# A chunked state-space scan and a gated feed-forward network on one core: the first loads in another order, GpSimd's scaling moved ahead of the second weights, a scan split in two

## The chip, the cores and the metric

The kernel runs on one core of a Trainium2 chip. A core has five engines with instruction queues of their own: TensorE (PE in the profile; its weight loads are listed as PEld), VectorE (DVE), ScalarE (ACT), GpSimd (POOL) and SyncE (SP, which here only starts transfers). Sixteen DMA engines move the data. The metric is the device time of one execution in microseconds; a lower time is better.

## The reference

There are two stages. The first is a recurrence over 768 tokens for each of 4 batches and 8 heads, with head dimension 32 and state dimension 16, written in chunks. The second is a feed-forward network with a ReLU gate over all 3072 tokens, of width 256 and inner width 1536.

```python
for c in range(nc):
    cum = np.cumsum(la, axis=-1)                               # la = log a in the chunk
    L = np.exp(cum[:, :, :, None] - cum[:, :, None, :]) * causal
    M = np.einsum('bhin,bhjn->bhij', Cc, Bc) * L
    y_intra = np.einsum('bhij,bhjd->bhid', M, xc)
    y_inter = np.einsum('bhin,bhnd->bhid', Cc, state) * np.exp(cum)[:, :, :, None]
    y[:, :, sl] = y_intra + y_inter
    Bx = np.einsum('bhjn,bhjd->bhjnd', Bc, xc) * decay_from_j[...]
    state = decay_full[:, :, None, None] * state + np.sum(Bx, axis=2)
...
gate = np.maximum(x @ w_gate, 0.0)      # x: y as 3072 tokens x 256
val = x @ w_val
return gate * val @ w_out
```

Inputs and output are float32 in HBM; the matmuls run on bfloat16 copies.

## The kernel before, in words

The kernel is free to choose its own chunk length and takes 128 tokens. Two chunks, 256 tokens of one batch with all 8 heads, are a *pair*; there are 12 pairs, three to a batch. Two pairs are a *block* of 512 tokens for the feed-forward network; there are 6 blocks. The feed-forward network of a block needs the recurrence of its two pairs, and the recurrence of the next pairs is woven between its matmuls, so that TensorE always has work.

The order of the work on each engine is the order of the program: `in_order` at the end ties each instruction to the one before it on its engine. Between engines only semaphores count. So the text of the kernel from line 620 on is a schedule, written by hand. Transfers are issued by SP (nearly all loads and stores), by ScalarE (four loads at the start) and by GpSimd (the weights, which are turned from float32 to bfloat16 on their way). An instruction that waits holds up all that stands behind it on its engine, a transfer's issue too.

The steps of a pair, with their lines in the kernel before:

- **Loads.** `load_bc` (L86) and `load_x` (L96) load B, C and x of the pairs 0 to 2, which are laid out in a special way ("wide"); `load` (L114, L115) loads the other pairs. `a_sb` (L134) is the decays of all batches, `a0` (L121) those of batch 0.
- **Scaling.** `scale_wide(p, j, engine)` (L276) multiplies C (j = 1) or B (j = 0) by decay factors `wfac` and writes the bfloat16 tile bs, in two instructions. Pair 0 is scaled on VectorE, pairs 1 and 2 on GpSimd. The factors are copied from PSUM for C, and made by a reciprocal for B. `cast_x` (L303) turns x to bfloat16 (xb).
- **Transposes.** `turn` and `transp` (L320) on TensorE, then `tevac` copies the result to BT (L335, L345) and, with a mask, to CT (L338 on ScalarE, L341 on VectorE).
- **Scores.** `G_wide` (L357) makes four PSUM banks of C times B. Two of them VectorE multiplies by the causal mask straight from PSUM (`gmask` with `True`, L370); the other two ScalarE copies to SBUF first (`gcopy`, L374), and `gmask` then masks them there.
- **State.** `adds` (L391) sums B times x of each chunk, `carry` (L410) and `pass_on` (L419) carry the state on with `dec`; `inter_wide` (L431) adds the state's part to y and `D_wide` (L445) the part within the chunk. `yevac_wide` (L455) copies y to yT, the input of the feed-forward network.
- **Feed-forward.** `gv` (L563, L566, 512 tokens) and `gvh` (L581, 256 tokens) do the gate and value products of 128 inner columns, ScalarE makes r by ReLU (L569, L584), VectorE makes h from r and the value product (L570, L587), and `fout` (L599) multiplies h by `wo`. PSUM has five shared banks, handed out in turn; a half-step `gvh` takes one, `gv` two, `G_wide` four.
- **Weights.** `weights(f0, f1)` (L192) issues wg and wv for the inner columns f0 to f1 of 12, `weights_out` (L196) all of wo. A one-element copy (`gate`, L634) that reads a factor holds the first of them back.
- **Decays of batches 1 to 3.** Two scans over `a_sb` (L232), a reciprocal and a multiply (`middle`, L238, L239), the matmuls of `decay` (L247).
- `keep_warm` (L183) runs matmuls on a tile of zeros whose result nobody reads.

Of the kernel before, what the change touches and what calls it, by code (L numbers as in the profile page):

```python
# [29 lines left out]
def kernel(  # L30
# [48 lines left out]
    def load_bc(p, j, *qs):  # L79
        s = st.setdefault(p, {})  # L80
        if "bcr" not in s:
            s["bcr"] = raw.tile([128, NH, 2, 2, N], FP32, tag="bcr", name="bcr")
        n = NH // len(qs)
        for i, q in enumerate(qs):
            hs = slice(i * n, (i + 1) * n)
            q.dma_start(  # L86
                out=s["bcr"][:, hs, j].rearrange("p h r n -> p h (r n)"),
                in_=(B, C)[j][0, hs, p * 256:(p + 1) * 256, :].rearrange(
                    "h (p r) n -> p h (r n)", r=2))

    def load_x(p, *qs):
        xr = raw.tile([128, NH, 2, D], FP32, tag="xr", name="xr")
        n = NH // len(qs)
        for i, q in enumerate(qs):
            hs = slice(i * n, (i + 1) * n)
            q.dma_start(out=xr[:, hs].rearrange("p h r d -> p h (r d)"),  # L96
                        in_=x[0, hs, p * 256:(p + 1) * 256, :].rearrange(
                            "h (p r) d -> p h (r d)", r=2))
        st.setdefault(p, {})["xr"] = xr

    def load(p):
        q = nc.sync
        if p < NWIDE:
            load_bc(p, 1, q)
            load_bc(p, 0, q)
            load_x(p, q)
            return
        b, c0 = p // PPB, 2 * (p % PPB)
        xr = raw.tile([128, 2, NH, D], FP32, tag="xr", name="xr")
        bcr = raw.tile([128, 2, 2, NH, N], FP32, tag="bcr", name="bcr")  # L110
        for i in range(2):
            sl = slice((c0 + i) * 128, (c0 + i + 1) * 128)
            for src, j in ((B, 0), (C, 1)):
                q.dma_start(out=bcr[:, i, j], in_=src[b, :, sl, :].rearrange("h s n -> s h n"))  # L114
            q.dma_start(out=xr[:, i], in_=x[b, :, sl, :].rearrange("h s d -> s h d"))  # L115
        st[p] = {"xr": xr, "bcr": bcr}
# [8 lines left out]
    nc.vector.memset(first, 0.0)  # L125
    load_bc(0, 1, nc.sync, nc.scalar)
    load_bc(0, 0, nc.sync, nc.scalar)
    load_bc(1, 1, nc.sync)
    load_bc(1, 0, nc.scalar)
    load_x(0, nc.sync, nc.scalar)  # L130
    nc.scalar.activation(first[:, 1:2], first[:, 0:1], AF.Relu)
    load_x(1, nc.sync)
    a_sb = glob.tile([2 * BH, H], FP32)
    nc.sync.dma_start(out=a_sb, in_=a.rearrange("b h (w s) -> (b h w) s", w=2))  # L134
    load(2)
    load(3)

    identf = const.tile([2 * BH, 2 * BH], FP32)
    make_identity(nc, identf)
# [37 lines left out]
    def keep_warm(n, tag="shared"):  # L177
        if tag == "tp":
            w = mm.tile([128, 128], FP32, tag="tp", name="w")
        else:  # L180
            w = bank("w", (128, 128))
        for _ in range(n):
            nc.tensor.matmul(out=w, lhsT=warm, rhs=warm, start=True, stop=True)  # L183
# [5 lines left out]
    def weights(f0, f1):  # L189
        fs = slice(f0 * 128, f1 * 128)  # L190
        for w, src in ((wg, moe_w_gate), (wv, moe_w_val)):
            nc.gpsimd.dma_start(  # L192
                out=w[:, :, fs], in_=src[:, fs].rearrange("(k p) f -> p k f", k=2))
# [74 lines left out]
    def scale_wide(p, j, eng):  # L268
        s = st[p]
        if "bs" not in s:  # L270
            s["bs"] = bs = att.tile([128, 4, 128], BF16, tag="bs", name="bs")
            s["tin"] = [[bs[:, 2 * j + r] for r in range(2)] for j in range(2)]
        src = s["bcr"].rearrange("s (t q) j r n -> s j r t q n", t=2)[:, j]
        f = wfac[:, j, :, :, p]
        for t in range(2):
            eng.tensor_tensor(  # L276
                out=s["bs"][:, 2 * j:2 * j + 2].rearrange(
                    "s k (q t n) -> s k t q n", q=4, t=2)[:, :, t],
                in0=src[:, :, t],
                in1=f[:, :, 4 * t:4 * t + 4].to_broadcast([128, 2, 4, N]),  # L280
                op=ALU.mult)
# [16 lines left out]
    def cast_x(p, ceng):  # L298
        s = st[p]
        cast = ceng.copy if ceng is nc.scalar else ceng.tensor_copy  # L300
        xb = att.tile([128, 2 * NH * D], BF16, tag="xb", name="xb")
        if p < NWIDE:
            cast(xb, s["xr"].rearrange("s h r d -> s (h r d)"))  # L303
            s["xb"] = xb.rearrange("s (h r d) -> s h r d", h=NH, r=2)
        else:
            cast(xb, s["xr"].rearrange("s i h d -> s (i h d)"))
            s["x"] = [xb[:, i * NH * D:(i + 1) * NH * D] for i in range(2)]

    def transp(p, k, apart=False):

        s = st[p]
        if "tp" not in s:
            s["tp"] = {}
        if apart and k == 0:
            s["tp"][k] = bank("tpb", (128, 2, 128), BF16)
        elif not s["tp"]:
            tp = mm.tile([128, 2, 2, 128], BF16, tag="tp", name="tp")
            s["tp"] = {0: tp[:, 0], 1: tp[:, 1]}
        for i in range(2):
            nc.tensor.transpose(out=s["tp"][k][:, i], in_=s["tin"][k][i], identity=ident)  # L320
# [61 lines left out]
    def adds(p):  # L382
        y_wide(p)
        s = st[p]
        s["A"] = [s["yw"][i][:, 256:320] for i in range(2)]
        halves = [i for i in range(2) if 2 * p + i < NC - 1]
        for r in range(2):
            for i in halves:
                half = slice(64 * i, 64 * i + 64)
                for q in range(4):  # L390
                    nc.tensor.matmul(  # L391
                        out=s["A"][i][32 * q:32 * q + 32],
                        lhsT=s["bs"][half, r, 32 * q:32 * q + 32],
                        rhs=s["xb"].rearrange("s (t q) r d -> s q r t d", t=2)[half, q, r],
                        start=r == 0, stop=True,
                        tile_position=(64 * i, 32 * q), skip_group_check=True)
        for i in halves:
            s["begun"][i] = True
# [4 lines left out]
    def carry(p, i):  # L403

        c = 2 * p + i
        T_[c] = n = att.tile([128, 2 * D], FP32, tag="T", name="T", bufs=3)
        if c == 0:
            nc.scalar.copy(out=n, in_=st[p]["A"][i])
        else:
            nc.vector.scalar_tensor_tensor(  # L410
                out=n, in0=T_.pop(c - 1), scalar=dec[:, c - 1:c], in1=st[p]["A"][i],
                op0=ALU.mult, op1=ALU.add)
# [8 lines left out]
    def inter_wide(p):  # L421
        s = st[p]
        for i in range(2):
            if 2 * p + i == 0:
                continue
            m = S.pop(2 * p + i)
            y = s["yw"][i][:, 0:256].rearrange("s (t m) -> s t m", t=2)
            for t in range(2):
                for q in range(4):
                    rows = slice(32 * q, 32 * q + 32)  # L430
                    nc.tensor.matmul(  # L431
                        out=y[rows, t], lhsT=m[rows, t], rhs=s["CT"][rows, t, i],
                        start=not s["begun"][i] and t == 0, stop=False,
                        tile_position=(32 * q, 32 * q), skip_group_check=True)
            s["begun"][i] = True
# [193 lines left out]
    decays(1)  # L629
    keep_warm(3)  # L630
    nc.vector.tensor_copy(wfac[:, 1], d)
    scale_wide(0, 1, V)
    nc.vector.reciprocal(wfac[:, 0, :, :, 0], wfac[:, 1, :, :, 0])
    nc.gpsimd.tensor_copy(gate[:, 0:1], wfac[0:1, 0, 0, 0, 0:1])  # L634
    weights(0, 4)
    weights(4, 8)
    scale_wide(0, 0, V)
    transp(0, 1, False)
    keep_warm(3)
    transp(0, 0, True)  # L640
    tevac(0, A_, V)
    nc.vector.reciprocal(wfac[:, 0, :, :, 1:3], wfac[:, 1, :, :, 1:3])
    keep_warm(4)
    G_wide(0)
    keep_warm(16)
    gcopy(0, 0)
    gmask(0, 2, V, True)
    gcopy(0, 1)
    gmask(0, 3, V, True)
    cast_x(0, A_)  # L650
    scale_wide(1, 1, P_)
    scale_wide(1, 0, P_)
    gmask(0, 0, V)
    gmask(0, 1, V)
    adds(0)
    keep_warm(5)
    pass_on(0, 0)
    carry(0, 0)
    inter_wide(0)
    D_wide(0)  # L660
    turn(1, True)
    yevac_wide(0, A_, V)
    carry(0, 1)
    cast_x(1, P_)
    tevac(1, V, A_)
    pass_on(0, 1)
    weights(8, NF)
    weights_out(0, NF)
    load(4)
    load(5)  # L670

# [22 lines left out]
    halves(0, 0, 6, 7)  # L694
    carry(1, 1)
    pass_on(1, 1)
    scan(0, H // 2)
    scan(H // 2, H)
    middle()
    scale_wide(2, 1, P_)  # L700
    scale_wide(2, 0, P_)
    make_upper_triangular(nc, maskUT[:, 0], 1.0, diag=True)
# [5 lines left out]
        nc.gpsimd.tensor_scalar_mul(smask[:, t], bd, tmask[:, t:t + 1])  # L708
    halves(0, 1, 0, 1, 2, 3, 4, 5, 6, 7)
    gv(0, 8)  # L710
    gv(0, 9)
    turn(2)
    tevac(2, V, A_)
    gv(0, 10)
    gv(0, 11)
    decay()
# [131 lines left out]
```

## Time and profile before

| | before |
|---|---|
| median of 4 runs | 131.12 us (130.99 to 131.62) |
| the profiled execution | 130.99 us, of which the profile's span is 129.1 us |
| TensorE busy | 121.5 us (94% of the span) |
| VectorE, ScalarE, GpSimd busy | 89.1, 81.5, 40.8 us |
| TensorE's granted clock | 1.00 over the whole span |
| read from HBM, written to HBM | 11.13 MB, 3.15 MB |

A busy time is the sum of an engine's instructions; it does not say whether anyone waited for them. A wait is the idle time of an engine ahead of an instruction, with the event that ended it. The chain that ended last follows the work back from the end of the span, at each step to what released it, so that what stands in it is what the time is made of.

### The profile page before, as it was taken

The page shows a single profiled execution, that of the slowest core. Times are in us where ns is not written, and L with a number is a line of the kernel's source. Part 1 is how long each engine was busy: PE and PEld are TensorE (multiplying, and loading weights), DVE is VectorE, ACT ScalarE, POOL GpSimd, SP SyncE. Part 2 cuts the span into 40 slices and gives each one's busy share as a digit, 9 for nine tenths or more (in the row PEclk, how much of TensorE's full clock was granted, in tenths as well). Part 3 has the DMA queues.
Part 4 walks back from the last instruction along what each step waited for, and adds up shares of the span by engine and source line. Part 5 has one row for each costly group of instructions (what it writes and reads, how often), then busy time and mean ns, then how long its engine had stood idle before and what let it go on. Part 6 is the DMA issues. An engine that isn't in the chain of part 4 may idle for free.

```text
span 129.1 us, 3441 instructions
## 1 busy us (share of the span) xinstructions
PE 121.5 (94%) x1290; PEld 84.9 (66%) x1296; DVE 89.1 (69%) x200; ACT 81.5 (63%) x185; POOL 40.8 (32%) x84
## 2 busy tenths in 40 slices
PE   6997797999999999999999999999999999999990
PEld 6774476568687567784567875477864677854770
DVE  4773979736599866578675878665789675688410
ACT  0565667565588854787844797935887745876310
POOL 6499346107193003580003750011930033000000
PEclk9999999999999999999999999999999999999999
DMA  4999999699895994289922197922200002200031
GB/s 68 187 212 215 225 202 187 80 105 118 95 207 74 127 115 48 81 145 119 106 42 76 37 149 93 110 33 89 81 0 0 0 5 81 81 0 5 0 111 52
DMA packets 72208, 12.14 MB, mean 94 GB/s; under 512 B 65936, under 2 KB 72192, under 8 KB 72192
## 3 DMA queue, kind: packets, MB, share of 16 engines
q1 hardware_dynamic: 66096, 8.91, 46.1%
q0 software_dynamic: 3184, 2.36, 11.8%
q10 hardware_dynamic: 2912, 0.66, 2.7%
q8 instruction: 10, 0.16, 0.5%
q14 instruction: 6, 0.05, 0.1%
HBM read 11.13 MB, written 3.15 MB: 111 GB/s over the span
## 4 chain that ended last, share of the span: by engine, by line
PE 83%; DMA 6%; DVE 3%; POOL 2%; ACT 1%; issue 1%; DVEq 0%
PE o L599 25%; PE gv L581 17%; PE val L566 15%; PE gate L563 13%; DMA wv<-in_moe_w_val_dram 6%; PE y L538 2%; PE g L464 2%; PE tp L320 2%; PE w L183 2%; PE A_ps L501 1%; PE y L527 1%; DVE h L587 1%; POOL wg L192 1%; DVE cp L232 1%; PE dec L247 1%
## 5 line engine op out<-in xcount | busy, mean ns | idle before, releaser
L599 PE MATMUL o<-wo,h 128*128 128x256 bf16 x288 | 34.7, 273 | 0.0
L570 DVE TENSOR_TENSOR h<-r,val 128x512 bf16<-128x512 bf16 x42 | 28.2, 684 | 8.8 <-ACT r L569 7.3
L599 PEld LDWEIGHTS <-h 128*128 128x128 bf16 x288 | 27.3, 98 | 5.0 <-issue 1.3
L587 DVE TENSOR_TENSOR h<-r,gv 128x256 bf16<-128x256 bf16 x60 | 23.8, 418 | 7.3 <-ACT r L584 6.7
L569 ACT ACTIVATE r<-gate 128x512 bf16<-128x512 f32 x42 | 24.6, 600 | 6.4 <-PE gate L563 5.0
L472 POOL TENSOR_SCALAR_AFFINE_SELECT gs<-gs 128x512 bf16<-128x512 bf16 (+1 forms) x18 | 9.0, 523 | 54.1 <-ACT gs L483 54.1
L566 PE MATMUL val<-yT,wv 128*128 128x512 bf16 x84 | 25.0, 379 | 0.3
L584 ACT ACTIVATE r<-gv 128x256 bf16<-128x256 f32 x60 | 22.5, 385 | 3.3 <-DVE h L587 0.8
L581 PE MATMUL gv<-yT,wg 128*128 128x256 bf16 x120 | 22.9, 273 | 1.3 <-DVE h L587 0.8
L581 PE MATMUL gv<-yT,wv 128*128 128x256 bf16 x120 | 22.9, 273 | 1.1 <-DMA wv<-in_moe_w_val_dram 1.1
L563 PE MATMUL gate<-yT,wg 128*128 128x512 bf16 x78 | 23.7, 379 | 0.0
L489 DVE TENSOR_TENSOR gs<-g,maskUT 128x512 bf16<-128x512 f32 x18 | 11.6, 686 | 10.4 <-issue 9.7
L566 PEld LDWEIGHTS <-wv 128*128 128x128 bf16 x84 | 8.2, 98 | 9.9
L581 PEld LDWEIGHTS <-wg 128*128 128x128 bf16 x120 | 11.2, 98 | 3.7 <-issue 1.8
L581 PEld LDWEIGHTS <-wv 128*128 128x128 bf16 x120 | 11.6, 98 | 3.0 <-DMA wv<-in_moe_w_val_dram 1.7
L563 PEld LDWEIGHTS <-wg 128*128 128x128 bf16 x84 | 7.8, 98 | 5.8
L290 POOL TENSOR_TENSOR bs<-bcr,scaleBC 128x256 bf16<-128x256 f32 x18 | 11.0, 632 | 0.0
L483 ACT CAST gs<-g 128x512 bf16<-128x512 f32 x9 | 5.3, 589 | 7.0 <-PE g L464 7.0
L615 ACT COPY ob<-o 128x512 f32<-128x512 f32 x10 | 5.8, 584 | 4.7 <-PE o L599 4.7
L551 ACT CAST yT<-y 128x512 bf16<-128x512 f32 x9 | 5.3, 586 | 5.5 <-PE y L538 5.3
L183 PE MATMUL w<-warm 128*128 128x128 bf16 x51 | 6.6, 311 | 1.1 <-DVE tmask L154 1.1
L183 PEld LDWEIGHTS <-warm 128*128 128x128 bf16 x51 | 5.2, 143 | 1.5 <-DVE tmask L154 1.0
(99 smaller groups left out, 118.9 us busy)
## 6 DMA issues: line engine op xcount, KB each, us to landing
out_dram<-ob SPq DMA_DIRECT2D x10, 256.0 KB, 2.2
xr<-in_x_dram SPq DMA_DIRECT2D x19, 128.0 KB, 3.6
bcr<-in_C_dram SPq DMA_DIRECT2D x19, 64.0 KB, 3.6
bcr<-in_B_dram SPq DMA_DIRECT2D x19, 64.0 KB, 3.7
wg<-in_moe_w_gate_dram POOLq DMA_DIRECT2D x3, 256.0 KB, 6.5
wv<-in_moe_w_val_dram POOLq DMA_DIRECT2D x3, 256.0 KB, 7.2
wo<-in_moe_w_out_dram POOLq DMA_DIRECT2D x1, 768.0 KB, 12.1
xr<-in_x_dram SPq DMA_DIRECT2D x2, 256.0 KB, 10.1
```

The lines of the kernel that those rows point to most:

```text
L183: nc.tensor.matmul(out=w, lhsT=warm, rhs=warm, start=True, stop=True)
L290: eng.tensor_tensor(out=bs.rearrange("s k (q t n) -> s k t q n", q=4, t=2)[:, :, t], in0=src[:, :, t], in1=f[:, :, 4 * t:4 * t + 4].to_bro ...
L472: nc.gpsimd.affine_select(out=dst, in_=dst, pattern=[[0, n], [1, 128]], compare_op=ALU.is_ge, fill=0.0, base=0, channel_multiplier=-1)
L489: nc.vector.tensor_tensor(out=d[:, q], in0=g[q], in1=m, op=ALU.mult)
L563: nc.tensor.matmul(out=g, lhsT=wg[:, k, fs], rhs=yT[:, k, tk], start=(k == 0), stop=(k == 1))
L566: nc.tensor.matmul(out=v, lhsT=wv[:, k, fs], rhs=yT[:, k, tk], start=(k == 0), stop=(k == 1))
L569: nc.scalar.activation(r, g, AF.Relu)
L570: nc.vector.tensor_tensor(out=fst[b][:, f], in0=r, in1=v, op=ALU.mult)
L581: nc.tensor.matmul(out=gv_[:, j], lhsT=w[:, k, fs], rhs=yT[:, k, tk], start=(k == 0), stop=(k == 1), skip_group_check=True)
L584: nc.scalar.activation(r, gv_[:, 0], AF.Relu)
L587: nc.vector.tensor_tensor(out=fst[b][:, f, u * 256:(u + 1) * 256], in0=r, in1=gv_[:, 1], op=ALU.mult)
L599: nc.tensor.matmul(out=o[:, ts % 2], lhsT=fst[b][:, f, ts * 128:(ts + 1) * 128], rhs=wo[:, f], start=(f == 0), stop=(f == NF - 1), skip_gr ...
```

## The change

The loads at the start come in another order. x of pair 0 goes ahead of B and C of pair 1. x of pair 1 and the loads of the pairs 2 and 3 are issued later: a one-element memset on VectorE, placed after the scaling of pair 0, must come before x of pair 1, and SP's queue is in order. The first quarter-set of weights (`weights(0, 4)`) is held by the copied factors in place of the reciprocal, so it is issued earlier. GpSimd scales pair 1 ahead of issuing `weights(4, 8)`; `weights(8, NF)` then stands ahead of its cast of x of pair 1. ScalarE casts x of pair 0 ahead of its two copies of scores, TensorE does the sums of pair 0 right after the scores, and one run of 19 warm matmuls stands in place of 16 and 5. The first half of the scan goes to the middle of pair 0, the second half and `middle` between `gv(0, 8)` and `gv(0, 9)`. The transposes of pair 2 are copied by ScalarE alone.

```diff
     def load_x(p, *qs):
         xr = raw.tile([128, NH, 2, D], FP32, tag="xr", name="xr")
+        if p == 1:
+            nc.vector.memset(xr[0:1, 0, 0, 0:1], 0.0)
...
     load_bc(0, 1, nc.sync, nc.scalar)
     load_bc(0, 0, nc.sync, nc.scalar)
+    load_x(0, nc.sync, nc.scalar)
     load_bc(1, 1, nc.sync)
     load_bc(1, 0, nc.scalar)
-    load_x(0, nc.sync, nc.scalar)
-    nc.scalar.activation(first[:, 1:2], first[:, 0:1], AF.Relu)
-    load_x(1, nc.sync)
     a_sb = glob.tile([2 * BH, H], FP32)
     nc.sync.dma_start(out=a_sb, in_=a.rearrange("b h (w s) -> (b h w) s", w=2))
-    load(2)
-    load(3)
+    nc.scalar.activation(first[:, 1:2], first[:, 0:1], AF.Relu)
...
     nc.vector.tensor_copy(wfac[:, 1], d)
+    nc.gpsimd.tensor_copy(gate[:, 0:1], wfac[0:1, 1, 0, 0, 0:1])
+    weights(0, 4)
     scale_wide(0, 1, V)
     nc.vector.reciprocal(wfac[:, 0, :, :, 0], wfac[:, 1, :, :, 0])
-    nc.gpsimd.tensor_copy(gate[:, 0:1], wfac[0:1, 0, 0, 0, 0:1])
-    weights(0, 4)
-    weights(4, 8)
     scale_wide(0, 0, V)
+    load_x(1, nc.sync)
+    load(2)
+    load(3)
     transp(0, 1, False)
     keep_warm(3)
     transp(0, 0, True)
     tevac(0, A_, V)
     nc.vector.reciprocal(wfac[:, 0, :, :, 1:3], wfac[:, 1, :, :, 1:3])
+    scale_wide(1, 1, P_)
+    scale_wide(1, 0, P_)
+    weights(4, 8)
+    cast_x(0, A_)
     keep_warm(4)
     G_wide(0)
-    keep_warm(16)
+    adds(0)
+    keep_warm(19)
     gcopy(0, 0)
     gmask(0, 2, V, True)
     gcopy(0, 1)
     gmask(0, 3, V, True)
-    cast_x(0, A_)
-    scale_wide(1, 1, P_)
-    scale_wide(1, 0, P_)
     gmask(0, 0, V)
     gmask(0, 1, V)
-    adds(0)
-    keep_warm(5)
     pass_on(0, 0)
     carry(0, 0)
+    scan(0, H // 2)
     inter_wide(0)
     D_wide(0)
     turn(1, True)
     yevac_wide(0, A_, V)
     carry(0, 1)
+    weights(8, NF)
     cast_x(1, P_)
+    weights_out(0, NF)
     tevac(1, V, A_)
     pass_on(0, 1)
-    weights(8, NF)
-    weights_out(0, NF)
     load(4)
     load(5)
...
     carry(1, 1)
     pass_on(1, 1)
-    scan(0, H // 2)
-    scan(H // 2, H)
-    middle()
     scale_wide(2, 1, P_)
     scale_wide(2, 0, P_)
...
     halves(0, 1, 0, 1, 2, 3, 4, 5, 6, 7)
     gv(0, 8)
+    scan(H // 2, H)
+    middle()
     gv(0, 9)
     turn(2)
-    tevac(2, V, A_)
+    tevac(2, A_, A_)
     gv(0, 10)
     gv(0, 11)
     decay()
```

## The prediction

> **What bounds the kernel now.** I read the page first (busy shares, then the chain that ended last), then the chain in order of time, the waits of the first 45 us, the timelines of GpSimd, VectorE and ScalarE, and the landings of single transfers.
>
> ```profile
> span 129.1 us, 3441 instructions
> ...
> PE 121.5 (94%) x1290; PEld 84.9 (66%) x1296; DVE 89.1 (69%) x200; ACT 81.5 (63%) x185; POOL 40.8 (32%) x84
> ...
> DMA  4999999699895994289922197922200002200031
> ```
>
> TensorE is busy in 94% of the span and from 23 us on it hardly stops. Only its gaps before that can be won. The DMA row is full in slices 2 to 6, that is from 3.2 to 19.4 us (a slice is 3.23 us), so there a load goes earlier only if another goes later. The chain (start, us, what) shows the gaps:
>
> ```profile
> 5.31 0.87 POOL wg L192
> 6.19 0.72 POOL wv L192
> 7.16 0.46 issue
> 7.62 8.17 DMA wv<-in_moe_w_val_dram
> 15.83 0.83 PE gv L581 x6
> 17.41 0.52 ACT yT L455 x2
> 18.40 0.80 DVE h L587 x2
> 19.39 0.47 DVE cp L232
> 19.88 0.62 DVE cp L232
> 21.32 1.47 PE gv L581 x12
> ```
>
> Two things set the end: the second `weights` transfer of wv (columns 4 to 8), issued at 7.62 and landed 8.17 us later, and VectorE's two scans, after which TensorE starts again at 21.32. The waits say the same (total us, times, longest):
>
> ```profile
> PE gv L581 <- DMA wv<-in_moe_w_val_dram: 1.1, 2, 0.7
> ...
> PE gv L581 <- DVE h L587: 0.8, 1, 0.8
> ```
>
> Of the two waits for wv one ends at 11.95 (first quarter, 6.19 + 5.7), one at 15.83 (second quarter). The wait for h is the one behind the scans.
>
> **Part 1, the scans.** Before, scan, scan, reciprocal and multiply stand on VectorE between the carry of pair 1 and the eight h products of the second half block, from 19.30 to 20.95. The sixth half-step of that block reuses the PSUM bank of the first and waits 0.82 us for its h. Moved, that work no longer stands there. What is late next: the first r (ScalarE, 19.68, behind the Sw that waits for the carry), its h at about 20.05, done 20.4, against the bank wanted at 20.34: under 0.1 us. Gain 0.8. The first scan now stands between pair 0's masks and its yT copy: 0.54 us, in a gap of VectorE of 0.59 (9.99 to 10.57) that grows if the masks end earlier; its a_sb landed at 9.4 with x of pair 1 ahead of it, now it is ahead of that x. Cost nothing; were the gap gone, up to 0.54. The second scan, reciprocal and multiply (0.61 + 0.15 + 0.23, with gaps 1.07) now stand between the h products of `gv(0, 8)` and `gv(0, 9)`. Behind them h(9) ends at 25.45 + 1.07 = 26.52 on the old clock, and `decay()` takes that PSUM bank; it began at 26.40, so TensorE loses up to 0.17 there (0 if VectorE runs ahead, as it may without the old backlog). h(11) is not late: the BT copy (0.28) has gone to ScalarE, which sat 0.97 us waiting for it. ScalarE then does BT 0.37 and CT 0.84 from about 24.8 to 26.0 and is free before its old 26.42. Sum of part 1: -0.82 + 0.17 = -0.65.
>
> **Part 2, the first weights.** The gate copy on GpSimd waited for the reciprocal (ends 4.94); now for the wfac copy (ends 4.25): 0.69 earlier, so wv's first quarter is issued at 5.50 and lands at 11.2 for 11.9. The first gv then runs at 11.2, its r is next held by ScalarE (CT and Sw until about 11.7), h at 12.2, and `G_wide(1)`, which needs that bank, at 12.6 in place of 13.27. So pair 1's masks, carry and Sw come 0.65 earlier: Sw ends at 15.66, and inter and D of pair 1 could run 0.65 earlier, if wv's second quarter allows.
>
> **Part 3, GpSimd's order.** The second quarter no longer follows at once; it stands behind four `scale_wide(1, ...)` instructions, which wait for C and B of pair 1. These now move behind x of pair 0, so 768 KB go ahead of the end of C, the amount that went ahead of the end of x of pair 0, which landed at 3.37 + 4.1 = 7.5. By the windows' GB/s (168, 169, 196, 176, 210 in the 1 us stretches from 2 us) 786 kB are through at 6.3 and the landing follows by some 0.8. So scaling starts between 7.1 and 7.5, takes 4 times 0.40 (minimum) to 1.90 in all, then wg takes 0.76 of GpSimd: wv is issued at 9.5 to 10.2, for 7.62.
>
> ```profile
> wv<-in_moe_w_val_dram POOLq DMA_DIRECT2D x1, 256.0 KB, 5.7
> ...
> wv<-in_moe_w_val_dram POOLq DMA_DIRECT2D x1, 256.0 KB, 8.2
> ```
>
> Its time to land is bounded by the rows: 5.1 (the first wg, alone on the queue), 5.7 (wv behind one transfer, as it will be), 8.2 (behind three). With 5.1 to 5.7 it lands at 14.6 to 15.9, for 15.8; I take 15.3, the middle, and 18.4 as the bad end. At 15.3 two half-steps of 0.44 remain, inter starts near 16.1 for 16.59: gain 0.5 of the possible 0.65.
>
> [...] No weight transfer here landed in under 5.1 us.
>
> Behind the weights on GpSimd: the third quarter (issued earlier than 10.76, nobody waits for it), then cast_x(1), at about 12.3 for 10.21. Who waits: `adds(1)` on TensorE, ready after `G_wide(1)` at 13.0. Cast ends 12.9, free; and 0.9 us later would still hide behind wv's second quarter. wo follows at 13 for 12.23; it landed at 24.3 and is read at 27.21: hidden.
>
> **Part 4, VectorE's masks of pair 0.** The masks from SBUF took 1.56 us beside GpSimd's scaling, and 0.75 in pair 1 with GpSimd idle:
>
> ```profile
> 8.43 1.56 DVE L370 TENSOR_TENSOR gs<-gs,wmask 128x512 bf16<-128x512 bf16 x2
> ...
> 8.36 1.90 POOL L276 TENSOR_TENSOR bs<-bcr,wfac 128x128 bf16<-128x128 f32 x4
> ...
> 14.99 0.75 DVE L370 TENSOR_TENSOR gs<-gs,wmask 128x512 bf16<-128x512 bf16 x2
> ```
>
> The masks from PSUM took 1.29 both with and without scaling beside them. Scaling from 7.3 to 9.1 still meets the SBUF masks from 8.5 on: they end between 9.3 and 9.9 for 9.99. TensorE sets the rest: its warm matmuls fall from 21 to 19 (16 took 1.62 in weight loads, 0.1 each), so D of pair 0 starts about 0.2 earlier, 9.77 for 9.97. That 0.2 is inside part 2's 0.65 (ScalarE free at 11.7 for 11.86) and not counted again; without it 0.65 becomes 0.5. cast_x(0) goes ahead of the gs copies on ScalarE, into an idle stretch of 0.76 for its 0.63; x of pair 0 is loaded earlier.
>
> [...]
>
> **Part 5, x of pair 1 and loads 2, 3.** A one-element memset on VectorE (0.06) after pair 0's scaling holds SP's queue from about 4.5 to 5.55. x of pair 1 takes the place of C of pair 2 (issued 5.62, landed 11.1) with twice its bytes: an estimate of 11 to 12.3, about when its cast comes up. B and x of pair 2 landed at 17.8 and 22.3 and are read by TensorE at 24.14 and 28.98, so 2 us are spare; pair 3's last part landed at 28.3, read at 30.88, 1.4 spare once the clock is 1.15 earlier.
>
> **Sum.** -0.65 (scans) - 0.5 (pair 1) = -1.15. The profiled execution took 130.99 with a span of 129.1, so 129.84; the median of the four is 131.12, 0.13 more: 130.0 us.
>
> **Rivals.** *The second quarter is the new wait (slower).* If it takes 8.2 us as its old self did, it lands at 9.9 + 8.2 = 18.1, pair 1's inter slips by 2.3, less 0.65: +1.6, 132.7; at 7.2 (median) 17.1, +0.6, 131.7. It decides for slower once wv lands after 15.8 + 0.65 = 16.45. For: the queue was full until 19 us. Against: its 8.2 came behind three transfers, now one. 0.2.
> *Pair 1 gains nothing.* wv lands at 15.8 as before: only the scans count, -0.65, 130.5. 0.14.
> *The scans' gain is handed back.* The second scan holds h(9) longer than reckoned, or another wait takes the gap's place: -0.4 to -0.5 from pair 1 alone, 130.65, which is no change. 0.12.
> That x of pair 1 is late would need a landing after 14.5; it is part of the first.
>
> **How the numbers follow.** A measurement tells 0.5% (0.66 us) from no change. Forecast 0.54 (own range 129.2 to 130.4). Faster: 0.51 of it and 0.09 of the second rival, 0.60. Same: 0.03, 0.05, 0.03 of the first rival, 0.12: 0.23. Slower 0.17. Range 129.1 to 131.7: to the slower rival at its median price; above it some 0.13 is left out, below 0.05.
>
> **What would show it.** Right: no wait of gv for h near 20 us; scaling of pair 1 at 7.1 to 7.5; wv's second quarter issued at 9.5 to 10.2, landed by 15.9; SBUF masks under 1.4; inter of pair 1 near 16.1. Wrong: that landing after 16.45, `adds(1)` waiting for GpSimd's cast, a wait of `decay()` over 0.3, or gaps of TensorE after 24 us.

## The result, and the profile after

The changed kernel takes 130.7 us (median of 45 executions, 130.2 to 132.95), the kernel before, run beside it, 131.28 us (71 executions, 130.77 to 133.03). The ratio is 0.9956, with an interval of 0.9943 to 0.9969: 0.58 us less, between 0.41 and 0.75. The forecast was 1.1 us less. Medians here are over all executions; the ratios leave out those that took over 1.5% longer than the fastest of their kernel (8 of the changed kernel, 7 of 12 in e4 below, its profiled one among them), so that a median and a ratio can differ.

The profiled execution took 130.46 us, with a span of 128.8 us. The head of its page, with the rows that answer to those of before:

```profile
span 128.8 us, 3440 instructions
...
PE 120.9 (94%) x1288; PEld 84.3 (65%) x1294; DVE 88.9 (69%) x200; ACT 81.8 (64%) x186; POOL 40.5 (31%) x84
...
DMA  4999999998998992299922188922200002200031
```

The busy times say almost nothing: TensorE is busy 0.6 us less, and the transfers stand about as dense as before. What changed is in the chain that ended last, from 4.6 us on (start, length, what):

```profile
4.62 0.87 POOL wg L191
...
5.50 0.72 POOL wv L191
6.22 1.31 issue
...
7.58 1.70 POOL bs L275 x4
9.27 0.70 POOL wg L191
9.98 6.27 DMA wv<-in_moe_w_val_dram
...
16.29 0.83 PE gv L580 x6
...
17.80 3.16 PE gv L580 x28
20.96 0.04 issue
21.01 1.47 PE gv L580 x12
```

Read from the bottom: VectorE's two scans, which stood ahead of the 21.32 us row before, are gone, and 28 matmuls run into the next 12 with a gap of 0.04 us. Read from the top: the chain now goes through GpSimd, which waits 1.3 us for C of pair 1, scales for 1.7 us, and only then issues the second quarter of wv, at 9.98 in place of 7.62. It lands at 16.25 in place of 15.8. The waits of TensorE have the same two facts:

```profile
PE gv L580 <- DMA wv<-in_moe_w_val_dram: 1.5, 2, 1.1
```

The 0.8 us wait for h is no longer listed, and the longer of the two waits for wv grew from 0.7 to 1.1 us. `D_wide(1)`, the last step of pair 1, starts at 17.39 for 16.92: 0.47 later. Its first line before:

```profile
16.92 0.24 PE L445 MATMUL y<-gs,xb 64*32 64x128 bf16 x4
```

And after:

```profile
17.39 0.24 PE L444 MATMUL y<-gs,xb 64*32 64x128 bf16 x4
```

So the change is the difference of a gain behind that point and a loss ahead of it.

That can be put in one figure that is used below: the span less the start of `D_wide(1)` is 129.1 - 16.92 = 112.2 us before and 128.8 - 17.39 = 111.4 us after. What stands behind pair 1 became 0.8 us shorter; what stands ahead of it 0.5 longer.

### The profile page after: what moved, and what is told of

Read it like the earlier page. It is cut to its first block, busy times and chain, and to the rows that moved or that the text cites. A ratio compares the mean times of both kernels' runs of the same rounds, so it can differ in the third digit from the quotient of the medians.

```text
span 128.8 us, 3440 instructions
## 1 busy us (share of the span) xinstructions
PE 120.9 (94%) x1288; PEld 84.3 (65%) x1294; DVE 88.9 (69%) x200; ACT 81.8 (64%) x186; POOL 40.5 (31%) x84
## 4 chain that ended last, share of the span: by engine, by line
PE 86%; DMA 5%; POOL 3%; issue 2%; DVE 1%; ACT 0%; DVEq 0%; POOLq 0%
PE o L598 25%; PE gv L580 20%; PE val L565 15%; PE gate L562 13%; DMA wv<-in_moe_w_val_dram 5%; PE y L537 2%; PE g L463 2%; PE tp L319 2%; PE w L182 2%; PE A_ps L500 1%; PE y L526 1%; POOL bs L275 1%; POOL wg L191 1%; PE dec L246 1%; POOL wv L191 1%
## 5 line engine op out<-in xcount | busy, mean ns | idle before, releaser
L488 DVE TENSOR_TENSOR gs<-g,maskUT 128x512 bf16<-128x512 f32 x18 | 11.6, 686 | 10.4 <-issue 9.7
L580 PEld LDWEIGHTS <-wg 128*128 128x128 bf16 x120 | 11.1, 98 | 3.5 <-issue 1.0
L182 PE MATMUL w<-warm 128*128 128x128 bf16 x49 | 5.7, 295 | 1.1 <-DVE tmask L153 1.1
L508 DVE TENSOR_TENSOR Sm<-A_ps,smask 128x256 bf16<-128x256 f32 x15 | 6.2, 412 | 0.0
## 6 DMA issues: line engine op xcount, KB each, us to landing
wo<-in_moe_w_out_dram POOLq DMA_DIRECT2D x1, 768.0 KB, 11.9
```

What stands on the lines that cost most here:

```text
L488: nc.vector.tensor_tensor(out=d[:, q], in0=g[q], in1=m, op=ALU.mult)
L580: nc.tensor.matmul(out=gv_[:, j], lhsT=w[:, k, fs], rhs=yT[:, k, tk], start=(k == 0), stop=(k == 1), skip_group_check=True)
```

## The experiments

Times are in us. "wv" is the issue and the landing of its second quarter, "D" the start of `D_wide(1)`; these and the span come from one profiled execution of each kernel.

| kernel | wv | D | span | span - D | median | ratio to before |
|---|---|---|---|---|---|---|
| before | 7.62, 15.8 | 16.92 | 129.1 | 112.2 | 131.28 | 1 |
| after | 9.98, 16.3 | 17.39 | 128.8 | 111.4 | 130.70 | 0.9956 (0.9943 to 0.9969) |
| e1 | 6.92, 15.2 | 16.37 | 127.8 | 111.4 | 129.52 | 0.9861 (0.9826 to 0.9895) |
| e2 | 7.68, 16.2 | 17.41 | 128.8 | 111.4 | 130.65 | 0.9942 (0.9915 to 0.9969) |
| e3 | 10.36, 17.1 | 18.22 | 131.2 | 113.0 | 132.25 | 1.0045 (1.0009 to 1.0081) |
| e4 | 10.21, 16.8 | 18.34 | 130.8 | 112.5 | 132.53 | 0.9955 (0.9917 to 0.9993) |
| e5 | 6.90, 15.0 | 16.12 | 127.5 | 111.4 | 129.39 | 0.9877 (0.9841 to 0.9913) |
| e6 | 6.91, 15.7 | 16.81 | 128.2 | 111.4 | 129.70 | 0.9885 (0.9862 to 0.9909) |
| e7 | 6.79, 15.1 | 16.57 | 130.0 | 113.4 | 131.12 | 0.9985 (0.9964 to 1.0007) |
| e8 | 9.17, 17.6 | 19.29 | 131.4 | 112.1 | 132.82 | 1.0086 (1.0057 to 1.0116) |
| e9 | 5.78, 14.5 | 20.22 | 132.4 | 112.2 | 133.84 | 1.0132 (1.008 to 1.0183) |
| e10 | 5.76, 14.2 | 17.98 | 129.3 | 111.3 | 131.23 | 0.9991 (0.9972 to 1.001) |
| e11 | 9.37, 17.5 | 18.64 | 130.8 | 112.2 | 132.73 | 1.0097 (1.0063 to 1.0132) |

The fifth column takes two values: 112.2 with the scans where they were (before, e8, e11) and 111.4 with the scans moved (after, e1, e2, e5, e6, e10). The exceptions each have a cause of their own that the trace shows: a halved clock that reaches past D in e3, e4 and e9, a wait for C of pair 2 in e7. So in these nine kernels the scans are worth 0.8 us whatever else is done, and the rest of the span is told by when pair 1 ends.

**e1: the second weights right behind the first.** It undoes one line of the change.

```diff
     weights(0, 4)
+    weights(4, 8)
     scale_wide(0, 1, V)
...
     scale_wide(1, 1, P_)
     scale_wide(1, 0, P_)
-    weights(4, 8)
```

> The changed kernel with one edit: weights(4, 8) is issued right behind weights(0, 4), ahead of GpSimd's scaling of pair 1, as in the kernel before. GpSimd idles 1.36 us there (6.22 to 7.58, waiting for C), so the two issues of 1.44 us cost the scaling 0.1 at most. Theory A (the second quarter of wv is issued too late, at 9.98): it is now issued near 6.9 and lands between 14.0 and 15.4 in place of 16.25; D of pair 1 starts at about 16.75 in place of 17.39, held then by the state chain (Sw ends 16.29); time 130.1 us, 0.6 under the changed kernel. Rival B (pair 1's masks, which meet the scaling of pair 2, hold pair 1 anyway): wv lands early, but D starts at 17.1 or later: 130.5. Rival C (the transfer is bound by what shares the DMA engines, not by its issue): it lands at 16 as before, 130.7.

The chain of this kernel that ended last:

```profile
6.92 8.32 DMA wv<-in_moe_w_val_dram
15.24 0.05 issue
15.28 0.83 PE gv L580 x6
```

Issued 3.06 us earlier than in the changed kernel, wv landed only 1.0 earlier, since it took 8.32 in place of 6.27; but `D_wide(1)` moved by the same 1.0 (17.39 to 16.37), and the time from a ratio of 0.9956 to 0.9861, which is 1.25 us. GpSimd lost little by it: its scaling starts at 7.73 (7.58 after), because the two issues fill a time in which it had waited for C of pair 1. D came 0.4 earlier than expected (16.75): C of pair 2 lands at 15.2 here, so the masks of pair 1 no longer meet its scaling and take 0.75 us in place of 1.24 (see e4). This is the version to keep; the line cost more than the whole change gained.

**e2: the scans alone**, in the kernel before.

```diff
     carry(0, 0)
+    scan(0, H // 2)
     inter_wide(0)
...
     pass_on(1, 1)
-    scan(0, H // 2)
-    scan(H // 2, H)
-    middle()
...
     gv(0, 8)
+    scan(H // 2, H)
+    middle()
     gv(0, 9)
     turn(2)
-    tevac(2, V, A_)
+    tevac(2, A_, A_)
```

> The kernel before with the scan part of the change alone: first scan behind carry(0, 0), second scan and middle between gv(0, 8) and gv(0, 9), transposes of pair 2 copied by ScalarE. By the prediction's part 1: the wait of gv for h near 20 us shrinks from 0.8 to under 0.2, decay waits 0.2 at most, time 0.65 to 0.8 us under before: 130.5 to 130.65. Rival (the gain exists only beside the rest of the change, or is handed back at decay): 131.1 to 131.3.

0.9942 is 0.76 us less (0.41 to 1.12): part 1 of the prediction said 0.65. The whole change with its 0.58 is not better than this part of it. One caution comes from this run: its wv was issued at 7.68, 0.06 later than before, and landed 0.45 later, and its first weight transfer took 6.0 us for 5.1, though nothing ahead of them was changed. Landings differ by that much between executions, so single profiles settle no difference of half a microsecond; the verdicts rest on the ratios.

**e3: the scans put back**, in the changed kernel (the diff of e2 turned round).

> The changed kernel with the scan part undone. Theory A: what is left is a loss, since pair 1's D starts 0.47 us later than before and nothing is won for it: 131.5 to 131.8 us, 0.3 to 0.5 over before. By the prediction's sum (0.5 won in pair 1): 130.8.

A ratio of 1.0045, above 1 by its whole interval: without the scans the change makes the kernel slower, by about 0.6 us. So the other parts, of which the prediction expected 0.5 of gain, lose. In its profile wv landed at 17.1, and TensorE then ran at half clock from 18.5 to 22.0 (see the clock, below). The loss does not need that: the five executions with a mean granted clock of 1.00 have a median of 132.02, 0.8 above the 131.18 of the 14 such executions of the kernel before beside them.

**e4: GpSimd scales pair 2 later**, behind the building of its masks. This tests the rival that VectorE's masks, not the weights, keep pair 1. The two instructions of VectorE and the two of GpSimd in the changed kernel's timelines (start, length, what, count, and in brackets the idle time ahead):

```profile
8.43 1.12 DVE L369 TENSOR_TENSOR gs<-gs,wmask 128x512 bf16<-128x512 bf16 x2
...
14.47 1.24 DVE L369 TENSOR_TENSOR gs<-gs,wmask 128x512 bf16<-128x512 bf16 x2
```

```profile
7.58 1.70 POOL L275 TENSOR_TENSOR bs<-bcr,wfac 128x128 bf16<-128x128 f32 x4 [1.36 <-DMA bcr<-in_C_dram]
...
13.72 1.71 POOL L275 TENSOR_TENSOR bs<-bcr,wfac 128x128 bf16<-128x128 f32 x4
```

B of pair 2 lands at 13.6 in the changed kernel (17.7 before; C at 13.1 for 11.1), so that GpSimd scales both from 13.7 to 15.4, on top of the masks of pair 1, which took 0.75 before and 1.24 now.

```diff
     pass_on(1, 1)
-    scale_wide(2, 1, P_)
-    scale_wide(2, 0, P_)
     make_upper_triangular(nc, maskUT[:, 0], 1.0, diag=True)
...
         nc.gpsimd.tensor_scalar_mul(smask[:, t], bd, tmask[:, t:t + 1])
+    scale_wide(2, 1, P_)
+    scale_wide(2, 0, P_)
```

> The changed kernel with GpSimd's mask building (the upper triangle, bd, smask) ahead of its scaling of pair 2, so that this scaling comes near 16.2 in place of 13.7 and does not meet the SBUF masks of pair 1. These should fall from 1.24 to about 0.75 us and Sw of pair 1 end about 0.4 earlier. Theory A: the late weights bind, so the time stays: 130.7. Rival B: D of pair 1 comes 0.4 earlier: 130.3.

The masks took 0.75 us again and the carry came 0.4 earlier (15.21 for 15.63), yet the ratio is 0.9955, that of the change itself. The collision is real and hidden: pair 1 waited for wv, which landed at 16.8 in this profile. (From 17.3 to 20.7 TensorE ran at half clock in it; what is read here lies ahead of that.)

**e5: e1, with the loads of the pairs 2 and 3 held** by a one-element memset behind the last mask of pair 0, to see whether other loads slow the weights.

```diff
     load_x(1, nc.sync)
-    load(2)
-    load(3)
...
     gmask(0, 1, V)
+    load(2)
+    load(3)
```

> The kernel of e1_weights_first with the loads of the pairs 2 and 3 held back further, by a one-element memset on VectorE behind pair 0's last mask (about 9.4 us in place of 5.4). In e1 wv's second quarter was issued at 6.92 and took 8.32 us to land, against 6.27 from 9.98 in the changed kernel. Theory S (its time to land is set by the other loads on the same DMA engines): it lands at 14 or earlier, D of pair 1 starts near 16.0 in place of 16.37, held then by VectorE's chain, time 0.3 under e1: 129.2 us. Theory Q (it is set by GpSimd's own queue, four weight transfers one behind the other): it lands at 15.2 as in e1, 129.5 us.

wv landed at 15.0 (15.2 in e1), and the ratio, 0.9877, can't be told from e1's. The loads of pair 2 now began at 9.69 in place of 5.93, so what they moved in these 4 us is not what kept the weights.

**e6: the loads as before**, the scans moved, and both weights held by the copied factors (0.7 us earlier than before).

```diff
     nc.vector.tensor_copy(wfac[:, 1], d)
+    nc.gpsimd.tensor_copy(gate[:, 0:1], wfac[0:1, 1, 0, 0, 0:1])
+    weights(0, 4)
+    weights(4, 8)
     scale_wide(0, 1, V)
     nc.vector.reciprocal(wfac[:, 0, :, :, 0], wfac[:, 1, :, :, 0])
-    nc.gpsimd.tensor_copy(gate[:, 0:1], wfac[0:1, 0, 0, 0, 0:1])
-    weights(0, 4)
-    weights(4, 8)
```

> The kernel before with its old load order, the scan part of the change, and the first gate on the copied factors with both first weight quarters behind it: so e1 without the new order of the loads, the new place of the cast of x of pair 0 and the single warm run. If the new load order is worth something it lies over e1: VectorE's SBUF masks of pair 0 meet GpSimd's scaling again (1.5 us), wv's first quarter lands after 11.9 in spite of its earlier issue: 130.2 to 130.5 us. If it is worth nothing: 129.5 us, as e1.

0.9885: the scans and the earlier gate, without any of the new load order, are worth 1.5 us of e1's 1.8. What the new order adds lies inside the intervals. It is not without effect on the weights, though: issued at the same time, 4.55, the first weight transfer took 5.6 us here and 4.5 in e1, the fourth 8.8 and 8.3.

**e7: e1, with the loads of the pairs 2 to 5 held** until the last mask of pair 1, so that for some 8 us only x of pair 1 is loaded beside the weights.

```diff
     load_x(1, nc.sync)
-    load(2)
-    load(3)
...
-    load(4)
-    load(5)
...
     gmask(1, 1, V)
+    load(2)
+    load(3)
+    load(4)
+    load(5)
```

> The kernel of e1_weights_first with the loads of the pairs 2 to 5 held until VectorE's last mask of pair 1 (about 15 us), so that from about 9 us on, when x of pair 1 is through, the weights have the DMA engines to themselves. Theory S: wv's second quarter lands at 13.5 or earlier (6.6 us or less after its issue). Theory Q: at about 15.2 again. The time is not the question here: the late loads of the pairs 2 and 3 may cost up to 2 us later; without such a cost 129.2 (S) or 129.5 (Q).

wv landed at 15.1, 0.1 before e1's, though the DMA engines moved 189 to 205 GB/s between 9 and 15 us where they moved 208 to 232 in e1: less was moved, and the weight queue went no faster. The test is weaker than it was meant to be, since x of pair 1 landed only at 13.5 (10.2 in e1), so that the weights were alone for the last 1.6 us. Theory S, by which the weights go faster with fewer loads beside them, is not borne out here: wv took 8.3 us from issue to landing, as in e1 (8.32). The time, 131.12, is lost later, as the waits of TensorE say: pair 2's C, issued too late, landed at 23.3.

```profile
PE tp L321 <- POOL bs L277: 1.7, 2, 1.2
```

**e8: the second weights behind the scaling, alone**, in the kernel before.

```diff
     weights(0, 4)
-    weights(4, 8)
...
     scale_wide(1, 1, P_)
     scale_wide(1, 0, P_)
+    weights(4, 8)
```

> The kernel before with one step of the change alone: weights(4, 8) is issued behind GpSimd's scaling of pair 1 in place of ahead of it. GpSimd then waits for C (landed at 7.05 before), scales until about 9.0 and issues wv near 9.8; with 6.3 to 6.7 us to land, as in the three profiles with this order so far, it lands at 16.1 to 16.5 for 15.8. Theory A (this step is the loss): D of pair 1 starts 0.3 to 0.7 later, time 131.6 to 132.0, 0.2 to 0.5% over before. Rival (the step costs nothing by itself, and e1 won by something else): the SBUF masks of pair 0 fall toward 1 us and the time is 131.0 to 131.3.

The chain of its profile has:

```profile
9.17 8.47 DMA wv<-in_moe_w_val_dram
```

1.0086, 1.1 us slower, about twice what was expected: wv was issued 1.55 later than before and landed 1.8 later (17.6), not less. Here the first weights are later than in the changed kernel, as they still wait for the reciprocal (wv's first quarter landed at 12.5, there at 11.4); so wv's second quarter, issued 0.8 earlier than there, landed 1.4 later. The sign is what counts: this one move is a loss by itself.

**e9: e1, with the first weights held only by the result of pair 0's scan**, to see whether a still earlier queue brings pair 1 further forward.

```diff
-    nc.gpsimd.tensor_copy(gate[:, 0:1], wfac[0:1, 1, 0, 0, 0:1])
+    nc.gpsimd.tensor_copy(gate[:, 0:1], cp0[0:1, 0:1])
```

> The kernel of e1_weights_first with the first gate reading the result of the first scan in place of the copied factors, so the four weight transfers are issued some 1.0 us earlier, from about 3.5 us on. Theory Q (the four run one behind the other at their own pace from the first issue): wv's second quarter lands at 14.1 to 14.4 in place of 15.2, TensorE no longer waits for it, and D of pair 1 is held by VectorE's chain, near 16.0: 129.2 us, 0.3 under e1. Rival (B, C and x of the pairs 0 and 1, which share the DMA engines, come later by as much): GpSimd's scaling of pair 1 or the cast of x of pair 0 waits longer, 129.5 us or more.

The rival is right in kind, by far more than its 129.5. wv did come earlier (14.5), but another load paid for it: x of pair 1, issued at 5.51 as in e1, now has three weight transfers issued ahead of it in place of two and landed at 15.2 in place of 10.2, as the chain and the waits show:

```profile
5.51 9.68 DMA xr<-in_x_dram
```

```profile
PE y L390 <- POOL xb L302: 3.2, 1, 3.2
```

TensorE stood for 3.2 us, and what followed was slower as well. The windows from 13 us on (stretch, its length, busy time and number of instructions of each engine, granted clock, DMA share, GB/s):

```profile
13.00:15.00 2.00, 0.00 (x0) 0.00 (x0) 1.81 (x4) 0.86 (x2) 0.00 (x0) 1.00 1.45 193
15.00:17.00 2.00, 1.09 (x21) 0.75 (x21) 0.28 (x1) 0.00 (x0) 1.73 (x3) 0.53 1.26 206
17.00:19.00 2.00, 2.00 (x11) 1.44 (x10) 0.84 (x2) 1.07 (x4) 0.97 (x3) 0.50 1.36 224
```

TensorE did nothing from 13 to 15, and from 15.1 to 22.0 its granted clock was 0.50.

**e10: e9 with the wait filled**, by warm matmuls whose result nobody reads.

```diff
     G_wide(1)
+    keep_warm(30, "tp")
     adds(1)
```

> The kernel of e9 with 30 warm matmuls (zeros, result unread) on TensorE between the scores and the sums of pair 1, where e9 left it idle from 12.8 to 15.9 us. In e9 the granted clock was 0.50 from 15.1 to 22.0 us. Theory H (the halving follows TensorE's idleness): the clock stays at 1.00, the work that took from 16.0 to 22.0 us at half clock takes some 3.5 us, so 2 to 2.6 us less than e9's 133.84: 131.2 to 131.8 us. Rival R (the halving has another cause, or costs nothing because something else was late then too): the clock still falls, or the time stays within 0.5 us of 133.84.

131.23 us, 2.6 less than e9, by 30 matmuls of zeros. The same windows:

```profile
13.00:15.00 2.00, 1.76 (x30) 1.67 (x31) 1.93 (x4) 1.07 (x2) 0.05 (x1) 1.00 1.45 197
15.00:17.00 2.00, 1.39 (x27) 1.23 (x27) 0.45 (x3) 0.51 (x2) 1.98 (x4) 1.00 1.26 203
17.00:19.00 2.00, 2.00 (x62) 1.47 (x60) 1.54 (x4) 1.69 (x6) 1.83 (x8) 1.00 1.37 231
```

x of pair 1 was cast at nearly the same time (14.95 for 15.26 in e9), so it is the clock that makes the difference: D starts at 17.98 for 20.22. Here the halved clock cost more than the late load, for which the 1.7 us from e1 to e10 stand.

**e11: e8 with its waits filled** in the same way.

```diff
         for j, w in ((0, wg), (1, wv)):
+            if (b, u, j) == (0, 0, 1) and f in (0, 4):
+                keep_warm(12, "tp")
...
+    keep_warm(5, "tp")
     halves(0, 0, 0, 1)
```

> The kernel of e8 with 5 warm matmuls ahead of the first feed-forward half-step of pair 1's stage and 12 each between the gate and the value products of its first and fifth half-step, where e8 waited for the weights (0.74, 0.98 and 0.43 us). In e8 the granted clock was 0.50 from 11.9 to 18.8 us. Theory H: the clock stays at 1.00. The late weights still land at 17.7; behind them only some 1.3 us of work ran at half clock, so D of pair 1 comes 0.6 us earlier than e8's 19.3, and the time is 132.2 us (e8: 132.82). Rival R: the clock falls all the same and the time is within 0.2 us of e8's or above it.

The clock stayed at 1.00, and D came at 18.64 as expected, 0.65 before that of e8's profile; but the medians are 132.73 and 132.82, no difference. e8's profiled execution, in which the clock was 0.50 from 11.9 to 18.8 us, took 133.19; most of its others had a shorter drop, by their mean granted clock of 0.987 for 0.974. So the clock does not explain e8's loss: with 1.00 throughout, e11 is still 1.3 us over the kernel before. The late weights do: 18.64 + 112.2 is 130.8, e11's span.

## Why the prediction was half right

**Part 1, the scans: right.** It summed 0.82 of gain and 0.17 of loss at `decay()`. The runs show 0.76 (e2) and 0.8 (the two values of span - D). The 0.17 did not come: h(9) ended at 25.83 for a forecast of 26.52, because VectorE runs ahead once its backlog is gone, which the prediction had named as the case of 0.

**Part 2, the first weights: nearly right.** Issued at 5.50 as forecast; wv's first quarter landed at 11.4 (forecast 11.2, before 11.9), and the bank wait of `G_wide(1)` ended at 12.76 (forecast 12.6, before 13.27). So pair 1 began 0.5 earlier.

**Part 3, GpSimd's order: the step that failed.** The scaling started at 7.58 and wv was issued at 9.98, both as forecast (7.1 to 7.5, where the 0.8 us from the bytes to the landing was an estimate, and 9.5 to 10.2). What failed is the next term: "With 5.1 to 5.7 it lands at 14.6 to 15.9". It took 6.27 and landed at 16.25; in e3 and e4, which issue it at the same place, 6.7 and 6.6. The rows for 5.1 and 5.7 were for a transfer with nothing or one ahead of it, and the prediction took them, since wv would now stand behind one ("as it will be"). Its own numbers spoke against that: part 2 had the first quarter of wv land at 11.2, and part 3 the second quarter issued at 10, so the first quarter and the second wg were both still ahead: two, not one. The row of before with two ahead is that of the second wg, issued at 6.91:

```profile
wg<-in_moe_w_gate_dram POOLq DMA_DIRECT2D x1, 256.0 KB, 7.7
```

By it wv would have landed at 17.7; the measured 6.27 lies between the rows, so the count alone does not give the landing either. What the runs show in its place is a pace of the whole train: in the eight kernels that issue the four transfers one right behind the other (before, e1, e2, e5, e6, e7, e9, e10) the fourth landed 10.4 to 11.1 us after the first was issued, whenever that was. Where the scaling stands in between (after, e3, e4, e8, e11) it took 11.7 to 12.5. The prediction's 15.3 was 10.7 us behind the first issue at 4.56, as if nothing stood in between. The shortest weight transfer after took 4.5 us (the first wg, issued 4.56, landed 9.06), the one that counted 6.27. In place of -0.5 this term measured +0.47 in the pair of profiles; by the ratios, after against e2, it is +0.2, and e3 against before +0.6. The sign is the same in all three, though the intervals of after and e2 overlap.

**Part 4, the masks: right for pair 0, missed for pair 1.** Pair 0's masks from SBUF took 1.12 (forecast under 1.4), D of pair 0, behind its first matmul, went on at 9.61 (forecast 9.77, before 9.97), and the first scan lay hidden behind them. But the prediction did not ask what else would come earlier: pair 2's B did, by 4 us, GpSimd scaled B and C on top of pair 1's masks, and the half microsecond that part 2 had gained was gone at the carry (15.63 for 15.66 before; Sw ended at 16.29 for 16.31). So even with wv at the forecast 15.3 the term could not have been -0.5. e4 shows that this cost lay hidden behind wv; without the late wv it would have been next in line. In e1 C of pair 2 comes later, at 15.2, and the collision with it is gone. Not every mask is slower for it: pair 1's masks with two SBUF inputs took 0.75 in e1, with GpSimd idle, and 1.24 after, beside the scaling; those with one input from PSUM took 1.29 in e1 (from 13.10, GpSimd idle) and 1.29 after (from 13.27, the scaling from 13.72 beside them).

**Part 5: right.** x of pair 1 landed at 10.2, before its cast. That it can be late, e7 and e9 show: issued within 0.1 us of the same time, it landed at 13.5 and 15.2.

**Sum and rivals.** By the two profiles the sum is -0.8 + 0.47 = -0.33, and the spans differ by 0.3. By the medians it is -0.58. The likeliest case, -1.15, did not occur; the second rival (only the scans count, 130.5) is nearest, with a little of the first in it: wv landed at 16.25, 0.2 short of the 16.45 from which the prediction let the first rival decide. That point was computed with a part 2 gain of 0.65 which the masks had already taken. The direction was right, by virtue of the scans alone, and 0.58 us is below the 0.66 that the prediction itself gave as the least that can be told from no change.

What stays open: what sets the pace of the weight queue. With its first transfer issued at 4.5 us and the other three behind it, the fourth was through at 15.0 to 15.2 in e1, e5 and e7, and at 15.7 in e6 with the old load order, which is within the scatter of one landing. No run tells whether the limit lies in the conversion to bfloat16, in GpSimd's part of the issue or in the engines.

## What to carry to other kernels

Before you choose a row for a transfer's time to land, count from your own forecast times how many of its queue are still in flight when it is issued; where a queue works off a train of transfers, look at the time from the first issue to the last landing too (here 10.4 to 11.1 us for four). Don't put a long transfer behind an instruction that waits (e8: 1.1 us lost by that move alone). When you pull loads forward, follow everything that they release, for an engine that starts earlier may run into another's instructions (here masks of 1.24 us in place of 0.75). Find the one event that the rest of the span hangs on (here the end of pair 1): the start of it plus a constant told the span of nine of these kernels within 0.1 us, and the constant moved by the part of the change behind it.

## What the hardware showed that was not expected

**The granted clock.** In four profiles, after waits of TensorE in the first 20 us, its clock went to 0.50 for 3.4 us (e3, 18.5 to 22.0; e4, 17.3 to 20.7) or 6.8 us (e8, 11.9 to 18.8; e9, 15.1 to 22.0), and in e9 that cost more than 2 us: e10, which fills the wait with warm matmuls, is 2.6 us faster, and x of pair 1 landed only 0.3 earlier in it. The waits ahead of it differ: 3.2 us in e9, but behind the start e3 had no wait above 1.8 us, e4 none above 1.1, e8 none above 1.0. And e2's profile, with waits of 0.5 and 1.0 us at the same place as e8's 0.7 and 1.0, stayed at 1.00, so these runs do not show which waits it follows.

**The weight queue.** Its transfers of the same size took 4.4 us (the first in e3) to 9.4 us (the sixth in e8), and issuing one 3 us earlier brought it 1 us earlier (e1).
